# Where the split tokens lie in on-chip memory: four small constants placed ahead of them, and a column offset for blocks of two tiles

## The chip, the core and the metric

The kernel runs on one core of one Trainium2 chip, in one launch. The metric is the device time of that launch in microseconds: 485.12 us is the median of three runs of the kernel before (484.73 to 485.75). The profile that is read below is of one further execution, which took 485.06 us; its trace spans 483.0 us from the first to the last instruction.

## The reference

For 2,048 tokens of width 448 the program computes one block of a conditioned network: six modulation vectors from a condition `c`, a normalised state-space convolution with a gated residual, and then a normalised, modulated feed-forward part with a gated residual. All of it is float32. Cut to what matters here:

```python
mod = (silu(c) @ w_mod)                       # sa, ca, ga, sb, cb, gb
h = layernorm(x) * (1 + ca) + sa
x = x + ga * ssm_conv(h)                      # long convolution over the 2048 tokens
h = layernorm(x) * (1 + cb) + sb
x = x + gb * ((silu(h @ w_gate) * (h @ w_up)) @ w_down)   # 448 -> 1792 -> 448
```

The last line is where nearly all matmuls lie, and the change touches the buffers that hold its `h`.

## The kernel before, in words

The 2,048 tokens are 16 tiles of 128 tokens. They are worked in six blocks (`BLOCKS = [2, 2, 3, 3, 3, 3]`): two blocks of two tiles (256 tokens), then four of three (384 tokens). For each block the modulated, normalised tokens are turned so that the 448 channels lie along the 128 partitions, in four groups `k` (the fourth holds the last 64 channels twice). Each is written as two float32r numbers, a rounded high part and what is left over: `hhi[:, k, :]` and `hlo[:, k, :]`, two buffers of 128 partitions by 4 groups by 384 columns (L140 and L141). These are the "tokens' parts". The function `parts` (L197) writes them, ACT the high part at L198 and DVE the low part at L199; for the first block the functions `high` and `low` do the same at L423 and L428. A block of two tiles uses columns 0 to 255 of each group, a block of three columns 0 to 383.

The feed-forward part runs over 14 slices `f` of 128 hidden units (function `ffn`, from L707). For each slice, `gate_up` forms the gate and the up product. Each is a sum of 11 matmuls in one PSUM bank: seven with `hhi` and four with `hlo` as the operand that streams through TensorE, 256 or 384 columns at a time, all at one line:

```python
pe.matmul(ps[s][:, 0:n], w[:, s, a], (hlo if lo else hhi)[:, k, 0:n], ...)      # L729
```

The stationary operand `w[:, s, a]` is a 128 by 128 piece of `wgu[f]` (named `gu` in the profile), the split weights. So a slice has 22 such matmuls, a block 308 and the program 1,848: 616 in the two blocks of two tiles, 1,232 in the four of three. Each has a different stationary operand from the one before, so that each matmul in the profile has a weight load (LDWEIGHTS, engine PEld) of its own, which runs beside the matmul before it. After the 22 matmuls of slice `f` come the down products of slice `f - 1` at L773: per tile of tokens three matmuls of 448 columns, where the split activations `phi` and `plo` are stationary and the split weights `wdh` and `wdl` stream through. In the last block the last two slices' down products are at L801.

All on-chip buffers are allocated in the order of the code, one behind the other, each at a multiple of 32 bytes in every partition. In the built program `hhi` begins at byte 48,544 and `hlo` at byte 54,688; the weights `gu` of slice 0 begin at byte 63,264, and the other slices' weights lie some whole number of times 512 bytes behind them. The step from one group `k` to the next is 1,536 bytes, and from one piece of weights to the next 512. So, counted modulo 512, every streaming operand of L729 begins at byte 416 and every stationary one at byte 288. At L773 the streaming `wdh` and `wdl` begin at 288 and 32, and the stationary `phi` and `plo` at 288. The matrix `tri` of the scan at L933 to L935 begins at 384.

The order of work is written out by hand in the code; nothing here is decided by a scheduler. The four constants of the change are columns of one number per partition: `ones`, `mhalf` (the exponent -0.5 of the normalisation, read by POOL at L168), `ntok` and `pick`. They are filled in the first microseconds.

Of the kernel before, what the change touches and what calls it, by code (L numbers as in the profile page):

```python
# [8 lines left out]
F32 = mybir.dt.float32  # L9
# [42 lines left out]
def f32(ap):  # L52
    return ap.bitcast(F32)
# [3 lines left out]
def tile_kernel(ctx, tc, x, a_re, a_im, b_re, b_im, c_re, c_im, log_dt,  # L57
                wd, wgate_up, states, groups, vecs, dft, idft, out):
    nc = tc.nc
    sy, ve, sc, po, pe = nc.sync, nc.vector, nc.scalar, nc.gpsimd, nc.tensor  # L60
    ctx.enter_context(tc.manual_schedule())

    const = ctx.enter_context(tc.tile_pool(name="const", bufs=1))
# [7 lines left out]
    def bank():  # L71
        t = psg.tile([128, 512], F32, name="bank")
        return t
# [38 lines left out]
    def split_d(j, part=None):  # L112
        hi, lo = wp[j]
        if not part:
            sc.copy(hi, wdn[j])
        if part != 0:
            ve.tensor_tensor(lo, wdn[j], f32(hi), op=OP.subtract)

    def split_w(j, part=None, en=ve):
        hi, lo, st = wgu[j][:, :, 0:3, :], wgu[j][:, :, 4:7, :], wgu[j][:, :, 3, :]  # L120
        w = raw[j]
        if not part:
            sc.copy(wgu[j][:, :, 0:4, :], w)  # L123
        if part is None or part == 1:
            en.tensor_tensor(lo, w[:, :, 0:3, :], f32(hi), op=OP.subtract)  # L125
        if part is None or part == 2:
            en.tensor_tensor(st[64:128], w[64:128, :, 3, :], f32(st[64:128]), op=OP.subtract)
# [9 lines left out]
    g0 = const.tile([128, D], F32)  # L137
    gm0 = const.tile([128, D], F32)
    gm1 = g0
    hhi = const.tile([128, 4, MB * 128], F32R)  # L140
    hlo = const.tile([128, 4, MB * 128], F32R)  # L141
    gd = const.tile([128, D], F32)
# [54 lines left out]
    def parts(hi, lo, src, k):  # L197
        sc.activation(hi, src, AF.Identity, bias=sbc[:, k:k + 1])  # L198
        ve.scalar_tensor_tensor(lo, src, sbc[:, k:k + 1], f32(hi), op0=OP.add, op1=OP.subtract)  # L199

    def transposes(ts):
        n = len(ts) * 128
        for k in range(4):
            ps = CV if k == 2 else bank()
            for j, i in enumerate(ts):
                pe.transpose(ps[:, j * 128:(j + 1) * 128], xn[i][:, k * 128:(k + 1) * 128], ident)  # L206
            parts(hhi[:, k, 0:n], hlo[:, k, 0:n], ps[:, 0:n], k)

    xd = [dram.tile([128, 512], F32, name=f"xd{q}") for q in range(MB)]

# [9 lines left out]
    def split_turned(ts):  # L220
        n, m = len(ts) * 128, len(ts)
        for k in range(4):
            hi, lo = (h[:, k, 0:n].rearrange("p (q a r) -> p q a r", q=m, a=4) for h in (hhi, hlo))
            parts(hi, lo, turned[:, 0:m, :, k, :], k)

    wp0 = ctx.enter_context(tc.tile_pool(name="wp0", bufs=1))
    ones = const.tile([128, 1], F32)
    mhalf = const.tile([128, 1], F32)
    ntok = const.tile([128, 1], F32)
    cs = const.tile([128, 5], F32)  # L230
    pick = const.tile([128, 1], F32)
    gac = const.tile([128, 4], F32)

    def mod_part(ps, w, ks):
# [34 lines left out]
    with tc.tile_pool(name="pre", bufs=1) as pre:  # L269
# [149 lines left out]

        def high(q, ks=range(4)):  # L420
            for k in ks:
                c_ = slice(q * 128, (q + 1) * 128)
                sc.activation(hhi[:, k, c_], pk[q][:, k * 128:(k + 1) * 128], AF.Identity, bias=sbc[:, k:k + 1])  # L423

        def low(q, ks=range(4)):
            for k in ks:
                c_ = slice(q * 128, (q + 1) * 128)
                ve.scalar_tensor_tensor(hlo[:, k, c_], pk[q][:, k * 128:(k + 1) * 128], sbc[:, k:k + 1], f32(hhi[:, k, c_]),  # L428
                                        op0=OP.add, op1=OP.subtract)

# [9 lines left out]
        def flag_of():  # L440
# [45 lines left out]
            **{f"r{q}": do(n2.root, [q]) for q in range(2)}, **{f"n1{q}": do(norm, q) for q in range(2)},  # L486
            **{f"xn{q}": (lambda q: lambda: sc.activation(h2[q], h2[q], AF.Copy, scale=n2.of[q][1]))(q) for q in range(2)},
            **{f"tr{q}": do(to_channels, q) for q in range(2)}, "hi1": do(high, 1),
            **{f"hi0{z}": do(high, 0, (2 * z, 2 * z + 1)) for z in range(2)},
            "lo1": do(low, 1),  # L490
            **{f"lo0{z}": do(low, 0, (2 * z, 2 * z + 1)) for z in range(2)},

            "w0": do(split_w, 0, 0), "w01": do(split_w, 0, 1, WV), "w02": do(split_w, 0, 2, WV),
# [211 lines left out]
    def run_blocks(pools, stages, first=None):  # L705
        work, hid = pools.work, pools.hid
        def ffn(ts, fresh, last, todo):  # L707
            n = len(ts) * 128
# [3 lines left out]
            def gate_up(f, nw):  # L712
                head = fresh and f < 2
                if fresh and f:
                    split_d(f)
                w = wgu[f]
                p = hid.tile([128, 256], F32, name="p") if fresh else p_of[f % 2]
                hi = hid.tile([128, MB * 128], F32R, name="phi")
                lo = hid.tile([128, MB * 128], F32R, name="plo")
                ps = [DN[2] if fresh and f == 0 else bank(), bank()]  # L720

                top = [(k, a) for k, ws in enumerate(((0, 4), (1, 5), (2, 6), (3,))) for a in ws]
                low = [(k, k) for k in range(4)]

                def mm(s, ka, lo, first=False, end=False):
                    for q, (k, a) in enumerate(ka):
                        pe.matmul(ps[s][:, 0:n], w[:, s, a], (hlo if lo else hhi)[:, k, 0:n],  # L729
                                  start=first and q == 0, stop=end and q == len(ka) - 1)  # L730

                if head:
                    for k in range(3):
                        for s in range(2):
                            mm(s, [(k, k)], False, k == 0)
                    for s in range(2):
                        mm(s, [(k, 4 + k) for k in range(3)] + [(3, 3)], False)
                    for s in range(2):
                        mm(s, low, True, False, True)
                else:  # L740
                    for s in range(2):
                        mm(s, top, False, True)
                        mm(s, low, True, False, True)
                sc.activation(p[:, 0:n], ps[0][:, 0:n], AF.Silu)  # L744
                pp[f] = hi, lo
                if last and f == NF - 1:
                    c_ = [slice(q * 128, (q + 1) * 128) for q in range(len(ts))]
                    for q in range(len(ts) + 1):
                        for o in c_[q:q + 1]:
                            ve.tensor_tensor(ps[1][:, o], p[:, o], ps[1][:, o], op=OP.mult)  # L750
                            sc.copy(hi[:, o], ps[1][:, o])
                        for o in c_[max(q - 1, 0):q]:
                            ve.tensor_tensor(lo[:, o], ps[1][:, o], f32(hi[:, o]), op=OP.subtract)
                    return
                if nw is not None:
                    split_w(nw, 0)
                ve.tensor_tensor(ps[1][:, 0:n], p[:, 0:n], ps[1][:, 0:n], op=OP.mult)  # L757
                if nw is not None:
                    split_w(nw, 1)
                sc.copy(hi[:, 0:n], ps[1][:, 0:n])  # L760
                ve.tensor_tensor(lo[:, 0:n], ps[1][:, 0:n], f32(hi[:, 0:n]), op=OP.subtract)  # L761
                if nw is not None:
                    split_w(nw, 2)
# [11 lines left out]
            m = len(ts) - 1  # L775
# [64 lines left out]
        if first is not None:  # L840
            for i in TILES[1]:
                load_x(i)
            for i in TILES[0]:
                first(i)
                n2.stat(i, TILES[0])
            n2.root(TILES[0])
            for q, i in enumerate(TILES[0]):
                make_xn(i, work.tile([128, 512], F32, name=f"xn{q}"))
            transposes(TILES[0])
        for b, ts in enumerate(TILES):  # L850
            todo = {}
            if b + 1 < len(TILES):
# [32 lines left out]
                if late:  # L885
                    go(late[0], n2.root, nx)
                    for q, (h, i) in enumerate(zip(late[1], nx)):
                        go(h, make_xn, i, xn_of[q])
                at(NF - 1, 0, transposes if late else split_turned, nx)
            ffn(ts, b == 0, b + 1 == len(TILES), todo)  # L890

# [154 lines left out]
def build(nc, aps, out):  # L1046
    with tile.TileContext(nc) as tc:
        a = dict(aps)
        tile_kernel(tc, a["A_u"].rearrange("b l d -> (b l) d"), *[a[n] for n in _INS[1:] + ["B_w_gate_up", "A_states", "w_mod_groups", "c_log_dt", "dft", "idft"]],
                    out.rearrange("b l d -> (b l) d"))  # L1050
# [20 lines left out]
```

## Time and profile before

| what | value |
|---|---|
| median of three runs | 485.12 us (484.73 to 485.75) |
| the profiled execution | 485.06 us |
| its span, first to last instruction | 483.0 us, so 2.06 us lie around it |
| granted TensorE clock over the span | 0.999 |
| PE busy | 471.6 us (98%) |
| PEld, DVE, ACT, POOL busy | 444.9, 285.1, 155.4, 59.8 us |
| share of PE in the chain that ended last | 92% |
| of it the matmuls of L729 / of L773 | 59% / 28% |

Times are microseconds, unless marked ns. PE is TensorE's matmul, PEld its weight load. The profile gives a matmul a duration that covers its way through the array; successive matmuls overlap, so what one costs is the distance from its start to the next one's. The chain of work that ended last gives that distance: a piece "PE bank L729 x22" is the time that 22 matmuls in a row held the chain. The view of one line gives the shortest, the median and the longest duration of its instructions in ns.

### The profile page before, as it was taken

What the parts mean: (1) busy time and instruction counts of PE and PEld (TensorE: products, weight loads), DVE (VectorE), ACT (ScalarE), POOL (GpSimd) and SP (SyncE); (2) the same over time, 40 slices, a digit from 0 to 9 for tenths busy, and PEclk for the clock granted to TensorE, in tenths of its full rate; (3) what the DMA queues carried; (4) which work ended last, traced back from release to release, by engine and by line L of the source; (5) the groups of instructions that cost most, each with busy time, mean ns of one, the idle gap of its engine ahead of it and who ended that gap; (6) DMA issues with size and microseconds to landing.
All of it is one profiled execution on the core that took longest, in us unless ns stands there. A gap on an engine that the chain in (4) does not pass through costs nothing.

```text
span 483.0 us, 7024 instructions
## 1 busy us (share of the span) xinstructions
PE 471.6 (98%) x2743; PEld 444.9 (92%) x2743; DVE 285.1 (59%) x550; ACT 155.4 (32%) x336; POOL 59.8 (12%) x82
## 2 busy tenths in 40 slices
PE   6999999999999999999999999999999999999995
PEld 4668988999999999999999999999999999999995
DVE  4879998768876546573644757375475544221225
ACT  5876545522234222332312323331222232112111
POOL 1220000000000040310022221002241000000000
PEclk9999999999999999999999999999999999999999
DMA  8965563020001200111200011130001112000001
GB/s 307 405 225 165 194 188 103 0 96 2 1 2 39 58 1 0 45 38 51 92 25 0 2 44 46 43 115 0 2 2 44 45 43 77 22 1 0 1 1 62
DMA packets 18778, 31.24 MB, mean 65 GB/s; under 512 B 2608, under 2 KB 13488, under 8 KB 18736
## 3 DMA queue, kind: packets, MB, share of 16 engines
q1 hardware_dynamic: 18000, 30.52, 18.8%
q8 instruction: 23, 0.38, 0.3%
q10 hardware_dynamic: 736, 0.19, 0.2%
q14 instruction: 19, 0.16, 0.1%
HBM read 24.61 MB, written 6.03 MB: 63 GB/s over the span
## 4 chain that ended last, share of the span: by engine, by line
PE 92%; DMA 3%; DVE 2%; ACT 1%; issue 0%; POOL 0%; SPq 0%; ACTq 0%; DVEq 0%
PE bank L729 59%; PE dn L773 28%; DMA wm<-in_w_mod_groups_dram 2%; DMA x<-in_A_u_dram 1%; PE bank L238 1%; PE dn L449 1%; PE bank L934 1%; PE cv L933 1%; PE cv L935 0%; PE bank L947 0%; DVE x L812 0%; PE bank L206 0%; PE cv L946 0%; PE cv L948 0%; ACT raw L195 0%
## 5 line engine op out<-in xcount | busy, mean ns | idle before, releaser
L729 PE MATMUL bank<-hhi,gu 128*128 128x384 f32 (+1 forms) x1169 | 211.3, 320 | 0.0
L729 PEld LDWEIGHTS bank<-hhi,gu 128*128 128x128 f32 x1169 | 191.2, 188 | 3.1 <-issue 0.7
L729 PE MATMUL bank<-hlo,gu 128*128 128x384 f32 (+1 forms) x668 | 131.8, 319 | 0.0
L757 DVE TENSOR_TENSOR bank<-raw,bank 128x384 f32<-128x384 f32 (+1 forms) x69 | 36.9, 534 | 125.0 <-PE bank L729 121.6
L729 PEld LDWEIGHTS bank<-hlo,gu 128*128 128x128 f32 x668 | 110.2, 188 | 0.0
L760 ACT CAST phi<-bank 128x384 fp32r<-128x384 f32 (+1 forms) x83 | 36.9, 444 | 141.6 <-DVE bank L757 141.6
L744 ACT ACTIVATE raw<-bank 128x384 f32<-128x384 f32 (+1 forms) x70 | 32.9, 470 | 123.0 <-PE bank L729 114.9
L761 DVE TENSOR_TENSOR plo<-bank,phi 128x384 fp32r<-128x384 f32 (+1 forms) x83 | 42.5, 512 | 37.1 <-ACT phi L760 37.1
L773 PE MATMUL dn<-wdh,phi 128*128 128x448 f32 x218 | 58.3, 368 | 0.6 <-DVE run L698 0.4
L773 PE MATMUL dn<-wdh,plo 128*128 128x448 f32 x218 | 57.7, 366 | 0.0
L773 PE MATMUL dn<-wdl,phi 128*128 128x448 f32 x218 | 57.6, 365 | 0.0
L773 PEld LDWEIGHTS dn<-wdl,phi 128*128 128x128 f32 x218 | 41.0, 188 | 3.4
L773 PEld LDWEIGHTS dn<-wdh,plo 128*128 128x128 f32 x218 | 40.9, 188 | 3.3
L773 PEld LDWEIGHTS dn<-wdh,phi 128*128 128x128 f32 x218 | 38.9, 188 | 2.9 <-DVE run L698 0.7
L167 POOL TENSOR_SCALAR rsb<-mvb 128x1 f32<-128x1 f32 (+2 forms) x13 | 4.6, 354 | 171.9 <-DVE mvb L151 171.9
L167 POOL TENSOR_SCALAR rsa<-mva 128x3 f32<-128x3 f32 (+1 forms) x6 | 2.4, 396 | 116.1 <-DVE mva L151 116.1
L123 ACT CAST gu<-raw 128x1024 fp32r<-128x1024 f32 x14 | 14.6, 1046 | 0.0
L125 DVE TENSOR_TENSOR gu<-raw,gu 128x768 fp32r<-128x768 f32 x14 | 13.3, 953 | 0.1
L922 DVE TENSOR_TENSOR vl<-m,vh 128x448 fp32r<-128x448 f32 x12 | 9.1, 757 | 6.7 <-ACT vh L921 6.1
L908 POOL TENSOR_TENSOR m<-m,gm 128x448 f32<-128x448 f32 x9 | 10.4, 1154 | 21.4 <-DVE m L184 17.5
L194 ACT ACTIVATE raw<-raw,rsb 128x64 f32<-128x64 f32 x14 | 4.8, 346 | 21.0 <-DVE raw L193 11.9
L927 POOL TENSOR_TENSOR m<-m,gd 128x448 f32<-128x448 f32 x9 | 11.6, 1284 | 0.0
(232 smaller groups left out, 411.0 us busy)
## 6 DMA issues: line engine op xcount, KB each, us to landing
raw<-in_B_w_gate_up_dram SPq DMA_DIRECT2D x14, 512.0 KB, 3.9
rawd<-in_B_w_down_dram SPq DMA_DIRECT2D x16, 224.0 KB, 4.1
x<-in_A_u_dram SPq DMA_DIRECT2D x12, 224.0 KB, 3.3
out_dram<-x SPq DMA_DIRECT2D x11, 224.0 KB, 2.0
xd<-raw SPq DMA_DIRECT2D x9, 256.0 KB, 2.0
raw<-xd SPq DMA_DIRECT2D x36, 64.0 KB, 2.0
wm<-in_w_mod_groups_dram SPq DMA_DIRECT2D x5, 448.0 KB, 8.2
wm<-in_w_mod_groups_dram SPq DMA_DIRECT2D x5, 336.0 KB, 8.2
```

Of the source, the lines that this page charges most:

```text
L123: sc.copy(wgu[j][:, :, 0:4, :], w)
L125: en.tensor_tensor(lo, w[:, :, 0:3, :], f32(hi), op=OP.subtract)
L167: po.tensor_scalar(rs[:, 0:n], self.mv[:, 0:n, 1], EPS, None, op0=OP.add)
L729: pe.matmul(ps[s][:, 0:n], w[:, s, a], (hlo if lo else hhi)[:, k, 0:n], start=first and q == 0, stop=end and q == len(ka) - 1)
L744: sc.activation(p[:, 0:n], ps[0][:, 0:n], AF.Silu)
L757: ve.tensor_tensor(ps[1][:, 0:n], p[:, 0:n], ps[1][:, 0:n], op=OP.mult)
L760: sc.copy(hi[:, 0:n], ps[1][:, 0:n])
L761: ve.tensor_tensor(lo[:, 0:n], ps[1][:, 0:n], f32(hi[:, 0:n]), op=OP.subtract)
L773: pe.matmul(dn[q][:, 0:D], u[:, cs], v, start=f == 0 and z == 0, stop=f == (NF - 3 if last else NF - 1) and z == 2)
L908: (ve if on_v else po).tensor_tensor(v, h, g, op=OP.mult)
L922: ve.tensor_tensor(vl, v0, f32(vh), op=OP.subtract)
L927: (ve if on_v else po).tensor_tensor(h, h, gd, op=OP.mult)
```

## The change

The four constants are allocated ahead of `hhi` and `hlo`, where before they stood behind them. Four times 32 bytes move `hhi` and `hlo`, and the three buffers directly behind them (`gd`, `sbc`, `flag`), up by 128 bytes, and `cs` up by 32; everything from `gac` on stays where it was. In addition blocks of two tiles keep their parts in columns 48 to 303 of each group, in place of 0 to 255: 192 bytes further. So in the built program, modulo 512, the streaming operands of L729 begin at byte 32 in blocks of three tiles and at byte 224 in blocks of two, with the stationary ones still at 288. Nothing else of the program differs: on each engine the same instructions stand in the same order, with the same waits.

```diff
+    ones = const.tile([128, 1], F32)
+    mhalf = const.tile([128, 1], F32)
+    ntok = const.tile([128, 1], F32)
+    pick = const.tile([128, 1], F32)
+
+    first_col = lambda n: 48 if n == 256 else 0
     hhi = const.tile([128, 4, MB * 128], F32R)
     hlo = const.tile([128, 4, MB * 128], F32R)
     gd = const.tile([128, D], F32)
...
+        c_ = slice(first_col(n), first_col(n) + n)
...
-            parts(hhi[:, k, 0:n], hlo[:, k, 0:n], ps[:, 0:n], k)
+            parts(hhi[:, k, c_], hlo[:, k, c_], ps[:, 0:n], k)
...
-            hi, lo = (h[:, k, 0:n].rearrange("p (q a r) -> p q a r", q=m, a=4) for h in (hhi, hlo))
+            hi, lo = (h[:, k, first_col(n):first_col(n) + n].rearrange("p (q a r) -> p q a r", q=m, a=4) for h in (hhi, hlo))
...
-    ones = const.tile([128, 1], F32)
-    mhalf = const.tile([128, 1], F32)
-    ntok = const.tile([128, 1], F32)
     cs = const.tile([128, 5], F32)
-    pick = const.tile([128, 1], F32)
...
         def high(q, ks=range(4)):
             for k in ks:
-                c_ = slice(q * 128, (q + 1) * 128)
+                c_ = slice(48 + q * 128, 176 + q * 128)
...
         def low(q, ks=range(4)):
             for k in ks:
-                c_ = slice(q * 128, (q + 1) * 128)
+                c_ = slice(48 + q * 128, 176 + q * 128)
...
-                        pe.matmul(ps[s][:, 0:n], w[:, s, a], (hlo if lo else hhi)[:, k, 0:n],
+                        pe.matmul(ps[s][:, 0:n], w[:, s, a], (hlo if lo else hhi)[:, k, first_col(n):first_col(n) + n],
                                   start=first and q == 0, stop=end and q == len(ka) - 1)
```

## The prediction, made before the changed kernel ran

> **What bounds the kernel now.** I read the page's busy shares first, then the chain of waits, and then one slice of each kind of block in the chain in order of time.
>
> ```profile
> span 483.0 us, 7024 instructions
> PE 471.6 (98%) x2743; PEld 444.9 (92%) x2743; DVE 285.1 (59%) x550; ACT 155.4 (32%) x336; POOL 59.8 (12%) x82
> ...
> PE 92%; DMA 3%; DVE 2%; ACT 1%; issue 0%; POOL 0%; SPq 0%; ACTq 0%; DVEq 0%
> ```
>
> TensorE holds 92% of the chain that ended last. A busy PE alone would not say so, since matmul durations overlap, but the chain counts from release to release. DVE, the next engine, is busy 59% of the span. So a nanosecond more or less on every matmul reaches the end almost undiminished. What one matmul costs is read from the chain in order of time. These are two slices of the first kind of block (two tiles, 256 columns), with a piece of the scan in between:
>
> ```profile
> 67.08 2.80 PE bank L729 x22
> 69.88 1.22 PE dn L773 x6
> 71.10 2.60 PE bank L729 x22
> 73.70 0.21 PE bank L945
> 73.91 0.76 PE cv L946 x2
> ```
>
> and this is one slice of the second kind (three tiles, 384 columns):
>
> ```profile
> 303.04 3.87 PE bank L729 x22
> 306.90 1.83 PE dn L773 x9
> 308.73 3.87 PE bank L729 x22
> ```
>
> Columns are the start, the length and what held the chain. A matmul of L729 with 384 columns costs 3.87 us / 22 = 175.9 ns, one with 256 columns 2.60 us / 22 = 118.2 ns, and one of L773 with 448 columns 1.83 us / 9 = 203.3 ns. The chain is tight: nothing stands between these pieces. L946 is a plain float32 matmul of 448 columns, and its two passes take 0.76 us, 380 ns each. If such a pass spends exactly two clocks on a column (my estimate; the row does not say it), a clock is 0.424 ns, and the bare streaming would be 163 ns for 384 columns, 109 ns for 256 and 190 ns for 448. The float32r matmuls are then about 13, 10 and 13 ns above bare streaming, each with its own weight load running beside it. Over 1,232 matmuls of 384 columns and 616 of 256 that is 16.0 + 6.2 = 22.2 us: all that a better place of an operand could ever give back.
>
> **The change part by part.** The instructions, their order and their waits are the same on every engine. Only byte positions move, so every price here is a duration that changes, and no instruction or DMA is added or moved past another.
>
> *The four constants, and gd, sbc, flag and cs.* Nothing but a start address changes for their few readers. I cost it at nothing: most are read by DVE and POOL instructions, and those two engines hold 2% and 0% of the chain (`pick` and `cs` are operands of a few matmuls in the first 33 us). If POOL's reading of `mhalf` became slower by a tenth, it would stay inside the time in which POOL is idle (88% of the span).
>
> *Writing the parts.* ACT at L198 and DVE at L199 write the same numbers 128 bytes further, or 320 bytes in blocks of two.
>
> ```profile
> 150.28 0.33 PE bank L206 x3
> 150.61 2.44 PE dn L773 x12
> 153.05 7.72 PE bank L729 x44
> ```
>
> Between two blocks the down products of the last slices (2.44 us here) stand in the chain while the parts are written, and the next block's matmuls follow without a gap. So I cost this at nothing, too; the cover would have to fall away before a slower write showed, and there are only five such seams.
>
> *Reading the parts, the one term that can count.* All 1,848 matmuls of L729 stream from another place relative to the weights that are loaded beside them: modulo 512 the distance from the stationary to the streaming operand is 128 now; it becomes 256 in blocks of three, and 448 in blocks of two. The trace of before has no row at those distances for L729, so the price has to be bounded. The view of L729 shows how much matmuls of one shape differ now, in a stretch of block 1 (256 columns) and of block 3 (384 columns); the three numbers are the shortest, the median and the longest duration in ns:
>
> ```profile
> L729 PE MATMUL bank<-hhi,gu x171: 274/281/287, 95.0 to 142.0; 128*128 128x256 f32 x171
> L729 PE MATMUL bank<-hlo,gu x96: 278/281/285, 95.9 to 140.4; 128*128 128x256 f32 x96
> ...
> L729 PE MATMUL bank<-hhi,gu x196: 334/337/343, 234.5 to 311.6; 128*128 128x384 f32 x196
> L729 PE MATMUL bank<-hlo,gu x110: 336/337/343, 235.7 to 311.9; 128*128 128x384 f32 x110
> ```
>
> All of these have the same relative place modulo 512, and still differ by up to 13 and 9 ns. Something in the meeting of the stream with the weight load costs a varying amount, and its share can shrink or grow when the two start from another distance. The ends: if every matmul became as quick as the fastest of its kind, three-tile blocks would gain 1,232 x 3 ns = 3.7 us and two-tile blocks 616 x 3 to 7 ns = 1.8 to 4.3 us, together 5.5 to 8.0 us. If every one became as slow as the slowest, they would lose 1,232 x 6 = 7.4 and 616 x 6 = 3.7, together 11.1 us. One row goes further down. In the scan, `vl` streams 448 columns while the next weights are loaded, mostly in 358 ns, and L773 streams the same shape in 365:
>
> ```profile
> L935 PE MATMUL cv<-vl,tri x12: 358/358/367, 116.1 to 376.8; 128*128 128x448 f32 x12
> ...
> L773 PE MATMUL dn<-wdl,phi x218: 358/365/369, 40.4 to 469.3; 128*128 128x448 f32 x109
> L773 PE MATMUL dn<-wdh,plo x218: 362/365/369, 40.8 to 469.9; 128*128 128x448 f32 x109
> ```
>
> There the streaming operand stands 256 bytes, modulo 512, from the next stationary one, the distance that three-tile blocks of L729 get. Seven ns on all 1,848 matmuls would be 12.9 us. Against it stands that `wdl` over `phi` at L773 has this very distance and a median of 365, as much as `wdh` over `plo` at distance 0; the short ones of L935 directly follow a load of `tri`, which starts from a different place. So the row shows that such a matmul can be had 7 ns cheaper, and not that the distance alone does it.
>
> I take a small gain, about half of the way from the median to the fastest: 1.5 ns for each three-tile matmul (half of 337 - 334), and 2 ns for each two-tile one (about half of the 3 to 7 ns). That is 1,232 x 1.5 = 1.85 us and 616 x 2 = 1.23 us, in sum 3.1 us. It is a choice between a gain of 12.9 us and a loss of 11.1, near the rows in the middle. The sum against the profiled execution: 485.06 - 3.1 = **482.0 us**; this execution stands 0.06 us below the median of the three runs, so the same number serves for the median.
>
> Nothing is late next: the engine that waits for these matmuls is ACT at L744 and DVE at L757, and both wait for PE, not PE for them.
>
> ```profile
> L757 DVE TENSOR_TENSOR bank<-raw,bank 128x384 f32<-128x384 f32 (+1 forms) x69 | 36.9, 534 | 125.0 <-PE bank L729 121.6
> L744 ACT ACTIVATE raw<-bank 128x384 f32<-128x384 f32 (+1 forms) x70 | 32.9, 470 | 123.0 <-PE bank L729 114.9
> ```
>
> DVE sits idle 121.6 us waiting for L729 ahead of its product, ACT 114.9 us; a few us less of that turn into nothing new.
>
> **A rule to weigh.** The rows say that a float32r matmul with a load beside it costs some 13 ns more than bare streaming. The Trainium skill, TensorE: Matmul & The Clock Gate, section "Step-by-step: what each phase is for", says the opposite of a collision: "Loading the next tile's weights doesn't steal SBUF read bandwidth from the running matmul", since PE has two read ports. By that rule the place of either operand could not matter, and the time would stay 485.1 us. This trace neither proves the cause of the 13 ns nor shows a matmul of L729 at another place. The rule is the first rival below.
>
> **The rivals.** *The place does not matter* (485.1 us, between 484.1 and 486.1). The surplus is then a fixed price of a weight load, and the scatter is a beat that evens out. For it speak the equal medians of L773 at distances 0 and 256, and the 256-column matmuls of the final down products at L801, which stream `wdh` and `wdl` at distances 0 and 256, too:
>
> ```profile
> L801 PE MATMUL cv<-wdl,phi x2: 282/282/282, 476.2 to 477.2; 128*128 128x256 f32 x2
> L801 PE MATMUL cv<-wdh,plo x2: 282/282/282, 476.4 to 477.3; 128*128 128x256 f32 x2
> ```
>
> 282 ns, where L729 has 281 at distance 128. Against it speaks L935, and that these are six matmuls. Distances that are not a multiple of 128, such as the 448 of two-tile blocks, are hardly seen.
>
> *The new places meet more often: slower* (487.6 us). The same mechanism with the other sign, at L729 alone. In three-tile blocks the surplus becomes slightly larger, +0.8 ns on 1,232 matmuls = 1.0 us; in two-tile blocks the new distance moves half of the way to the slowest, about 2.5 ns on 616 = 1.5 us. It decides as soon as the three-tile median is at 338 and the two-tile one at 283 or more. For it speaks that the slowest lie twice as far from the median as the fastest in three-tile blocks (343, 337, 334): most phases have more to lose than to win. Against it speaks L935.
>
> *A large gain* (about 475 us): most of the L935 step, 5.5 ns, on all 1,848 matmuls is 10.2 us. It needs one distance to be good for the whole load, which the equal medians of L773 contradict.
>
> That the change does not do what it says can hardly be: the positions are fixed in the built program.
>
> **How the numbers follow.** A measurement of this kernel can tell about 0.2%, or 1 us, from no change. I give the small gain 0.45 (477 to 484.1 us), the large one 0.10, no effect 0.18 and the slower case 0.27, of which 0.07 lie above 488. The small gain is likeliest because the spread inside one shape shows that the meeting of stream and load has a price that is not fixed, and one row shows it lower. Faster by over 0.2% is then 0.45 + 0.10 = 0.55, within 0.2% 0.18, slower 0.27. The range of 477 to 488 us leaves out the large gain and the far end of the loss, 0.17 in all; the forecast's own range is 477 to 484.1.
>
> **What would show it.** In the profile of the changed kernel the chain's pieces of 22 matmuls should shrink from 3.87 to about 3.84 us in blocks of three, and from 2.60 to about 2.56 us in blocks of two; the medians of L729 go to about 335.5 and 279. L773 must stay at a median of 365, since none of its operands moves, and L198 and L199 at their durations. I am wrong if the medians of L729 stay at 337 and 281 (no effect), if either rises, or if the time moves while L729 does not: then something other than the reading of the parts is at work.

## The result and the profile after

The changed kernel took **481.91 us** (median of six runs, 480.99 to 483.51), the kernel before 485.09 us in six runs of its own. The ratio is 0.9937, with a 95% interval of 0.9920 to 0.9954: faster by 0.6%. The forecast was 482.0 us. The profiled execution took 480.99 us, the fastest of the six, with a span of 479.0 us; 0.9 us of what the two profiles differ by is therefore scatter between runs, and 0.6 us of it lies ahead of the first gate matmul, which starts at 33.0 us in place of 33.5 (in the profiles of the other kernels below it starts anywhere from 33.3 to 34.4).

The busy shares and the chain of waits after the change are almost those of before. The six inserted lines move L729 to L732, L773 to L776, L935 to L938.

```profile
PE 469.2 (98%) x2743; PEld 440.7 (92%) x2743; DVE 284.9 (59%) x550; ACT 155.2 (32%) x336; POOL 59.4 (12%) x82
...
PE 93%; DMA 3%; DVE 1%; ACT 1%; issue 0%; SPq 0%; ACTq 0%; DVEq 0%
```

TensorE bounds as before, and only its matmuls have other prices. The chain in order of time, first in a block of two tiles and then in a block of three:

```profile
69.87 2.52 PE bank L732 x22
```

```profile
231.89 7.63 PE bank L732 x44
239.52 1.85 PE dn L776 x9
```

22 matmuls of 256 columns take 2.52 us in place of 2.60, and 44 of 384 columns 7.63 us in place of 2 x 3.87 = 7.74. But nine down products, of which no operand moved, take 1.85 us in place of 1.83. The views of the two lines, shortest, median and longest duration in ns: L732 in a stretch of block 1 and one of block 3, as in the prediction, and L776 over the whole run:

```profile
L732 PE MATMUL bank<-hhi,gu x177: 276/277/285, 93.8 to 141.0; 128*128 128x256 f32 x177
...
L732 PE MATMUL bank<-hlo,gu x100: 276/277/285, 94.1 to 140.3; 128*128 128x256 f32 x100
```

```profile
L732 PE MATMUL bank<-hhi,gu x190: 333/334/347, 232.8 to 308.4; 128*128 128x384 f32 x190
...
L732 PE MATMUL bank<-hlo,gu x111: 334/334/339, 232.9 to 308.9; 128*128 128x384 f32 x111
```

```profile
L776 PE MATMUL dn<-wdl,phi x218: 362/368/372, 39.9 to 465.3; 128*128 128x448 f32 x109
...
L776 PE MATMUL dn<-wdh,plo x218: 358/368/371, 40.3 to 465.9; 128*128 128x448 f32 x109
```

Before, the medians were 281, 337 and 365. Not only is the median of the gate and up products lower, it now nearly coincides with the shortest: where the starts before followed each other in a beat (in one three-tile block: 173, 174, 175, 182, 176 ns, over and over), after the change they run at 173, 173, 174.

The two-tile blocks are less even than one piece shows. Within one block of the changed kernel, with all operands in one and the same place, twelve slices can be read alone by their starts. 22 matmuls take 2.50 to 2.52 us in seven of them and 2.59 in the five that begin between 115 and 131 us:

```profile
110.91 2.52 PE bank L732 x22
...
115.25 2.59 PE bank L732 x22
...
139.31 2.51 PE bank L732 x22
```

From the starts of successive matmuls, leaving out steps of over 215 ns (seams and waits), the mean price is, in ns:

| matmul | before | after | x count | us |
|---|---|---|---|---|
| gate and up, two tiles (256 columns) | 118.9 | 115.1 | 616 | -2.3 |
| gate and up, three tiles (384 columns) | 176.0 | 173.7 | 1,232 | -2.8 |
| down (448 columns) | 203.4 | 205.4 | 654 | +1.3 |

Together that is -3.8 us; the left-out steps in the blocks give back 0.4, and with the 0.6 us ahead of the first gate matmul it makes the 4.0 us between the two spans. In three-tile blocks alone the down products go from 203.3 to 205.7 ns; that number is used from here on.

### The profile page after: what moved, and what is told of

It reads as the page before. It is cut to its first block, busy times and chain, and to the rows that moved or that the text cites. A ratio compares the mean times of both kernels' runs of the same rounds, so it can differ in the third digit from the quotient of the medians.

```text
span 479.0 us, 7024 instructions
## 1 busy us (share of the span) xinstructions
PE 469.2 (98%) x2743; PEld 440.7 (92%) x2743; DVE 284.9 (59%) x550; ACT 155.2 (32%) x336; POOL 59.4 (12%) x82
## 4 chain that ended last, share of the span: by engine, by line
PE 93%; DMA 3%; DVE 1%; ACT 1%; issue 0%; SPq 0%; ACTq 0%; DVEq 0%
PE bank L732 58%; PE dn L776 28%; DMA wm<-in_w_mod_groups_dram 2%; DMA x<-in_A_u_dram 1%; PE dn L452 1%; PE bank L241 1%; PE bank L937 1%; PE cv L936 1%; PE cv L938 0%; PE bank L950 0%; PE bank L251 0%; PE bank L377 0%; DVE x L815 0%; PE bank L213 0%; PE cv L951 0%; PE cv L949 0%
## 5 line engine op out<-in xcount | busy, mean ns | idle before, releaser
L732 PE MATMUL bank<-hhi,gu 128*128 128x384 f32 (+1 forms) x1169 | 208.1, 316 | 0.0
L732 PEld LDWEIGHTS bank<-hhi,gu 128*128 128x128 f32 x1169 | 189.1, 188 | 3.4 <-issue 0.7
L732 PE MATMUL bank<-hlo,gu 128*128 128x384 f32 (+1 forms) x668 | 129.7, 316 | 0.0
L760 DVE TENSOR_TENSOR bank<-raw,bank 128x384 f32<-128x384 f32 (+1 forms) x69 | 36.9, 534 | 122.8 <-PE bank L732 119.1
L732 PEld LDWEIGHTS bank<-hlo,gu 128*128 128x128 f32 x668 | 108.4, 188 | 0.0
L776 PE MATMUL dn<-wdh,phi 128*128 128x448 f32 x218 | 58.6, 369 | 0.6 <-DVE run L701 0.5
L776 PE MATMUL dn<-wdh,plo 128*128 128x448 f32 x218 | 58.2, 368 | 0.0
L776 PE MATMUL dn<-wdl,phi 128*128 128x448 f32 x218 | 58.1, 367 | 0.0
L776 PEld LDWEIGHTS dn<-wdl,phi 128*128 128x128 f32 x218 | 40.9, 188 | 3.9
L776 PEld LDWEIGHTS dn<-wdh,plo 128*128 128x128 f32 x218 | 40.9, 188 | 3.9
L776 PEld LDWEIGHTS dn<-wdh,phi 128*128 128x128 f32 x218 | 38.6, 188 | 2.9 <-DVE run L701 0.7
L173 POOL TENSOR_SCALAR rsa<-mva 128x3 f32<-128x3 f32 (+1 forms) x6 | 2.4, 397 | 115.2 <-DVE mva L157 115.2
```

Of the source, the lines that this page charges most:

```text
L173: po.tensor_scalar(rs[:, 0:n], self.mv[:, 0:n, 1], EPS, None, op0=OP.add)
L776: pe.matmul(dn[q][:, 0:D], u[:, cs], v, start=f == 0 and z == 0, stop=f == (NF - 3 if last else NF - 1) and z == 2)
```

## The experiments

Below, **distance** is the byte at which the streaming operand begins less that of the stationary one, modulo 512, as laid out in the built programs. Two theories stood at the start. By the distance theory the price of a matmul is set by this number, since the stream meets the weight load that runs beside it. By the place theory it is set by where the streaming operand lies in itself. A third says that any move disturbs the beat and nothing follows from a number. All means are taken as in the table above.

**The two parts of the change alone.** First the constants without the column offset:

```diff
-    first_col = lambda n: 48 if n == 256 else 0
+    first_col = lambda n: 0
...
```

> The constants lie ahead (streaming parts 128 bytes further), but two-tile blocks begin at column 0 again. Distance modulo 512 from weights to parts: 256 in all blocks. Distance theory (a matmul's price is set by the distance between its streaming operand and the weights loaded beside it): three-tile pieces of 22 stay at the changed kernel's 3.82 us; two-tile pieces leave the changed kernel's 2.50 us, to an unknown value between 2.49 and 2.72. If 256 is good for any width: 2.50 and about 482 us. Place theory (the absolute place of the streaming operand alone sets it): the same three-tile pieces, two-tile unknown. Luck theory (any move breaks the beat and nothing follows from the distance): three-tile pieces anywhere from 3.80 to 3.90.

Measured: 484.21 us, ratio 0.9977 (0.9968 to 0.9987). Three-tile matmuls at 173.7 ns, as in the changed kernel; two-tile ones at 119.9, a little worse than before. So the same 128 bytes that help 384 columns do not help 256. The chain in a block of two tiles, and in one of three:

```profile
49.48 2.63 PE bank L732 x22
```

```profile
244.55 3.82 PE bank L732 x22
248.37 1.85 PE dn L776 x9
```

Then the 48 columns without the constants, which stand behind the parts again:

> Columns 48 to 303 in two-tile blocks, but the constants behind the parts as before. Distances: 128 in three-tile blocks as before, 320 in two-tile ones. Distance theory: three-tile pieces of 22 back at 3.87 us, and the down products beside them back at 1.83 us for nine; two-tile pieces between 2.49 and 2.72 us; in all about 483 to 485.5 us. Luck theory: three-tile pieces need not come back to 3.87.

Measured: 484.99 us, ratio 0.9995 (0.9980 to 1.0009). Three-tile matmuls are back at 176.0 ns and the down products between them at 203.3; two-tile ones, now at distance 320, have 117.9:

```profile
49.76 2.59 PE bank L731 x22
...
244.61 3.87 PE bank L731 x22
```

The offset of 48 columns is thus worth 1 ns by itself and 4.8 ns on top of the 128 bytes: it is not the column that counts, but where the sum ends. The granted clock is no rival: it was 0.997 with the constants alone and 1.000 with the columns alone, where three-tile matmuls are the slower ones.

**A whole 512 bytes.** In the kernel before, the identity matrix is allocated behind the parts:

```diff
-    ident = const.tile([128, 128], F32)
     tri = const.tile([128, 128], F32R)
...
     hlo = const.tile([128, 4, MB * 128], F32R)
+    ident = const.tile([128, 128], F32)
```

> The kernel before with the 128 by 128 identity allocated behind the parts, so that the parts move down by exactly 512 bytes; every distance modulo 512 is as before. Distance theory with a period of 512 bytes or a divisor of it: all pieces as before (3.87, 2.61, 1.83 us) and 485.1 us within 0.5. Place theory with a longer period, or luck: other values, by up to 3 us.

Measured: 485.04 us, ratio 1.0001 (0.9986 to 1.0016). The means are 119.0, 176.0 and 203.3 ns, and the beat of the three-tile blocks runs through the same values. Moving the parts does nothing if it is by 512 bytes:

```profile
49.00 2.61 PE bank L729 x22
...
244.24 3.87 PE bank L729 x22
```

**Moving the weights instead.** The changed kernel, with its parts where the change put them, and everything behind them 128 bytes further:

```diff
     gac = const.tile([128, 4], F32)
+    pad = const.tile([128, 32], F32, name="pad")
```

> The changed kernel with 128 unused bytes ahead of all weights and the split activations. The parts stay where the change put them (32 and 224 modulo 512), and everything that is stationary at the gate and up products moves 128 bytes, so the distances are 128 and 320, as in the kernel with the columns alone. Distance theory: three-tile pieces go back to 3.87 us, two-tile ones to the value of that kernel, the time as there (483 to 485.5 us). Place theory: pieces stay at 3.82 and 2.50 us and the time near 481.9.

Measured: 484.69 us, ratio 0.9993 (0.9984 to 1.0003). The gain is gone, with the parts at their new place:

```profile
244.09 3.88 PE bank L733 x22
247.97 1.82 PE dn L777 x9
```

Three-tile matmuls cost 176.2 ns and two-tile ones 118.1, within 0.2 ns of the values that distances 128 and 320 have in the kernels before and with the columns alone, and not those of the place (173.7 and 115.1). The place theory falls here, and the luck theory with it: three kernels that set distance 128 in three-tile blocks, each in another way, came back to 176.0, 176.0 and 176.2 ns. The split down weights and the split activations moved along with the weights here; the activations are moved alone further below, the split down weights nowhere.

**A scan of distances.** Four kernels, each run once and profiled in that run, beside one run of the kernel before at 485.33 us. `gd` goes ahead of the parts for 256 bytes, the constants for 128, unused columns ahead of the weights or of the split activations take 64 to 128 off, and the two blocks of two tiles each get a column of their own, so that a kernel tries up to four distances:

```diff
-    first_col = lambda n: 48 if n == 256 else 0
+    gd = const.tile([128, D], F32)
+    first_col = lambda ts: {0: 16, 2: 48}.get(ts[0], 0)
...
```

> The constants and gd ahead of the parts: distance 0 in three-tile blocks; the first block begins at column 16 (distance 64), the second at column 48 (192). The down products' operands keep their distances of 0 and 256. If the distance counts modulo 256, three-tile pieces are 3.82 us as at 256, and the second block's 2.50 to 2.53 us as at 448; the first block's about 2.60 as at 320. If it counts modulo 512, these may be anything between 3.76 and 3.90 and between 2.46 and 2.66. Carry-over theory (a down product's price depends on the beat that the gate and up products leave): nine down products take 1.85 us if the three-tile pieces are locked at one even value, 1.83 if they beat; own-distance theory: 1.83 whatever the gate and up products do, which the runs so far speak against.

Measured: 482.70 us. Three tiles at 0: 173.8 ns, the same as at 256, with down products at 205.7, again the same. Two tiles at 64: 118.0, as at 320; at 192: 115.9, about as at 448. All three pairs say that the distance counts modulo 256. The three-tile piece:

```profile
243.20 3.82 PE bank L732 x22
```

> gd ahead of the parts, the constants behind: distance 384 in three-tile blocks and in the first block, 480 in the second (column 24). The split activations lie 64 bytes further from the split down weights: distances at the down products 448 and 192. Modulo 256: three-tile pieces 3.87 us and the first block 2.61 as at 128; the second block near the 2.50 of 448 if a good place is wide, near 2.6 if it is narrow. Down products: own-distance theory expects another value than 203.5 ns, between 193 and 210; carry-over alone expects 203.5 as beside every three-tile beat so far.

Measured: 484.59 us. In a block of three:

```profile
244.42 3.87 PE bank L731 x22
```

At 384, three tiles 175.9 and two tiles 119.2, both as at 128, a fourth pair. At 480, two tiles 118.2: 32 bytes beside 448 most of the gain is gone. The down products at 448 and 192 cost 201.9 ns, less than in any kernel up to here, though the three-tile matmuls beside them beat as before.

> The constants ahead and 64 unused bytes ahead of the weights: distance 192 in three-tile blocks; first block at column 80 (distance 0), second at column 56 (416). Split activations 128 bytes further: distances 384 and 128 at the down products. If a place that is good for one width is good for the other, three-tile pieces fall below 3.82 us here, as 448 (the same modulo 256) did for two tiles; if each width has its own, they stay between 3.82 and 3.90. First block: 2.63 as at 256 if the period is 256. Second block: between 2.50 and 2.60, beside 448. Down products 193 to 210 ns by their own distance, 203.5 or 205.5 by carry-over alone.

Measured: 483.61 us. Three tiles at 192: 174.4; two tiles at 0: 120.1, at 416: 119.1. The place that is best for 256 columns is neither the best nor the worst for 384. Down products at 384 and 128: 203.4 ns.

> gd ahead, the constants behind, 64 unused bytes ahead of the weights: distance 320 in three-tile blocks; the first block at column 36 (464), the second at column 28 (432), 16 bytes to either side of 448. Split activations 96 bytes further: distances 416 and 160 at the down products. A wide good place: 2.50 us in both blocks; a narrow one: above 2.55 on one side at least. Three-tile pieces between 3.76 and 3.90 us: distance 320 gave two tiles a value between the best and the worst, so about 3.85. Down products as in the two kernels with other distances there.

Measured: 480.89 us. In a block of three:

```profile
243.04 3.81 PE bank L732 x22
```

Three tiles at 320: 173.4, steady, the lowest found; my "about 3.85" for their pieces was a miss, since two tiles have only a middling value at this distance. Two tiles at 464: 117.6, at 432: 119.0. So 16 bytes to either side of 448 cost most of the gain or all of it. Down products at 416 and 160: 201.7.

**The best of each.** Three-tile distance 320, two-tile 448, down products 416 and 160:

```diff
+    gd = const.tile([128, D], F32)
+    first_col = lambda ts: {0: 32, 2: 32}.get(ts[0], 0)
...
+    pad = const.tile([128, 16], F32, name="pad")
...
+            self.gap.tile([128, 24], F32, name="gap")
```

The first two lines replace those of the changed kernel, with the four constants behind the parts again; `pad` stands ahead of the weights and `gap` ahead of the split activations.

> The best distance found for each of the three kinds of matmul, counted modulo 256: 64 in three-tile blocks (320), 192 in two-tile blocks (448, column 32), 160 at the down products (416 and 160). Distance theory: two-tile pieces of 22 at 2.50 to 2.53 us, three-tile ones at 3.82, nine down products at 1.81 to 1.82; two blocks shorter by about 1.3 us in all than in the kernel with columns 36 and 28, so about 479.5 us, faster than the changed kernel by 2 to 3 us. If the gains don't add up (each good place moves the beat of its neighbour), about 481 us.

Measured: **479.64 us**, ratio 0.9882 (0.9863 to 0.9901), below the changed kernel's interval. In its trace the starts in a block of two tiles, gate and up products from 100.95 to 103.48:

```profile
100.95 0.98 PE L732 MATMUL bank<-hhi,gu 128*128 128x256 f32 x7
...
103.48 0.57 PE L776 MATMUL dn<-wdh,phi 128*128 128x448 f32 x2
```

2.53 us for 22. And in a block of three, from the chain:

```profile
241.81 3.81 PE bank L732 x22
245.63 1.82 PE dn L776 x9
```

The means are 115.2 and 173.4 ns for gate and up products, and 201.7 for the down products. The gains add up: about 479.5 us was expected.

**Where the slower down products come from.** Two kernels differ from this one in the place of the split activations alone.

> As the kernel with the best distances, but the split activations 64 bytes lower: distances 480 and 224 at the down products (224 modulo 256). Own-distance theory: another value than 201.6 ns there, between 198 and 206, with the gate and up pieces as in the kernel with the best distances. Nothing known says better or worse.

Measured: 480.53 us, ratio 0.9900 (0.9875 to 0.9924); down products 204.1 ns, the gate and up products beside them 173.5. The down products, too, have a price by their own distance: 160 gives 201.7, 224 gives 204.1.

> As the kernel with the best distances, but without the bytes ahead of the split activations: distances 0 and 256 at the down products, as in the kernels before and changed. Gate and up products as in the kernel with the best distances (locked at 173.4 ns). Carry-over theory: down products at 205.5 ns as beside every locked three-tile piece at these distances, nine of them 1.85 us, and the time 654 x 3.9 ns = 2.5 us above the kernel with the best distances. If the slower down products came from the distance 256 or 0 of the gate and up products and not from the locked beat: 203.5 ns and 1.2 us above.

Measured: 479.79 us, ratio 0.9903 (0.9870 to 0.9936). The gate and up products are as even as in the best kernel, but the down products do not cost 205.5 ns. In the view of their line, in three-tile blocks:

```profile
L776 PE MATMUL dn<-wdl,phi x38: 362/365/369, 240.2 to 309.9; 128*128 128x448 f32 x38
...
L776 PE MATMUL dn<-wdh,plo x36: 362/365/368, 240.8 to 305.0; 128*128 128x448 f32 x36
```

Their mean is 202.1 ns. My carry-over theory as I had put it, that an even run of the matmuls ahead makes the down products dear, falls: 173.4 ns and even, and still cheap. So does the other reading with 203.5.

The starts show what the two prices are made of. In the changed kernel, in blocks of three, the first of nine down products takes 201 ns and each of the other eight 206 or 207; in this kernel, with the same distances of 0 and 256 and the same even run ahead, they go round 201, 202, 203, 199, 207, 203, 202, 203, 199. So the down products have a beat of their own, and it can lock, too, but here at a dear value.

## Why the prediction was right, and where not

*The bound and the only term.* Both held. The instructions and waits are the same, PE holds 93% of the chain, and what is not scatter lies in what a matmul costs. The writing of the parts stayed as it was: the high part's 384-column form has a median of 606 ns before and after, the low part's 612 and 614.

*The mechanism.* The prediction took the scatter within one shape as a sign that the meeting of stream and weight load has a price that can change with the distance. The four runs on the parts and on the moves of 512 and 128 bytes show that the distance sets it in three-tile blocks, where every kernel at one distance has the same mean within 0.3 ns. In two-tile blocks the distance decides which values can occur, and not always which of them does: 2.50 and 2.59 us for 22 stand in one block. That it is the weights and not the split activations is shown: moving the latter by 64 or 96 bytes left the three-tile matmuls at 173.4 to 173.5 ns. Whether it is the load beside the matmul that is met, or the matmul's own earlier one, cannot be told within a slice, where both lie at the same place modulo 256. The last matmul of a slice tells more: the load that runs beside it is that of `phi`. From its start to that of the first down product it is 173 to 174 ns in three-tile blocks of the kernel with the best distances and of the one without bytes ahead of the split activations, but 180 in every slice of the one with `phi` 64 bytes lower, though the six steps before it are 173 to 174 in all three. So the place of the load beside it counts for that step. By which mechanism stays open.

*The sizes.* Three-tile matmuls were forecast to gain 1.5 ns and gained 2.3; two-tile ones 2 and gained 3.8. Both are nearer to the whole step from the median to the fastest (3, and 3 to 7 ns) than to half of it, because in the starts of the changed kernel the beat locks at a low value (173 to 174 ns, in most two-tile slices 113 to 114) and no longer visits the slow ones. The two-tile mean of 115.1 ns takes in the slices at 2.59 us. With these two terms alone, 2.8 + 2.3 = 5.1 us, the profiled time of before would have become 480.0 us. Of the 22.2 us that the prediction estimated as the most that places could give back, the best kernel here reached 5.4 (485.02 us for the kernel before beside it, less 479.64).

*The step that failed* is the sentence that L773 must stay at a median of 365 since none of its operands moves. It went to 368, and 654 times 2.0 ns gave back 1.3 of the 5.1 us that the gate and up products gained. The right total comes from gains that were taken too small and a loss that was left out, so that it was met to 0.1 us is luck. A down product's price hangs on its own distance and on that of the matmuls ahead of it: in three-tile blocks, at the same own distances of 0 and 256, it is 202.7 to 203.3 ns behind distance 128, 205.7 behind 0 or 256, and 202.1 behind 320. What it is that one line hands to the next stays open: the even steps ahead are 173 to 174 ns in the changed kernel and in the one at 202.1 alike. The signs that the prediction named, the median durations, are not the price either. In the kernel with the best distances the median is 336 ns, above the changed kernel's 334, though its matmuls follow each other faster (173.4 against 173.7 ns):

```profile
L732 PE MATMUL bank<-hhi,gu x168: 336/336/338, 241.6 to 308.4; 128*128 128x384 f32 x168
```

*The rivals.* "The place does not matter" is refuted by the four runs above. It leaned on equal medians at distances 0 and 256, and on L801 at the same two; with a period of 256 bytes these are one distance, and the argument had compared a place with itself. With its parts at the same place, a 384-column matmul costs 173.7 or 176.2 ns by the place of its weights. The Trainium skill (TensorE: Matmul & The Clock Gate, "Step-by-step: what each phase is for") says that loading the next tile's weights takes no SBUF read bandwidth from the running matmul. What the prediction drew from that, that the place of either operand could not matter, does not hold for these float32r matmuls; whether read bandwidth is what they share is not shown. "Slower" was right in one thing: the constants alone do make two-tile matmuls slower, by 1.0 ns at distance 256, and it is the column offset that turns this round. The row of L935, which the prediction gave as a hint, has not moved:

```profile
L938 PE MATMUL cv<-vl,tri x12: 358/358/369, 113.7 to 373.3; 128*128 128x448 f32 x12
```

Its operands were not moved either, so it says nothing on the cause.

## What to carry to other kernels

Where a stream of float32r matmuls bounds and each has its own weight load, read the distance between the starts of successive matmuls; a repeating uneven beat above the bare streaming time (163 ns for 384 columns by the prediction's estimate) is worth a scan of where the streaming operand begins relative to the weights, in steps of 16 to 32 bytes over 256, for each width apart. Align nothing by feel: the best place for one width is an ordinary one for another, and a good place can make the next line's matmuls dearer, so the sum is what to measure. Read the slices one by one, too, since one mean can cover two values. And before two equal rows are read as "no effect", make sure that they differ in the quantity in question modulo its likely period.

## What the runs showed of the hardware that was not expected

The mean step from start to start, in ns, by distance modulo 256. A range is over several kernels or blocks.

| distance | 256 columns | 384 columns |
|---|---|---|
| 0 | 119.8 to 120.1 | 173.7 to 173.8 |
| 64 | 117.8 to 118.3 | 173.4 to 173.5 |
| 128 | 118.9 to 119.2 | 175.9 to 176.2 |
| 160, 176 | 119.1, 119.0 | not tried |
| 192 | 114.8 to 116.3 | 174.4 |
| 208, 224 | 117.6, 118.2 | not tried |

At some distances a block settles at one even value and at others it goes round a beat of several values. At 192 the 256-column matmuls have both: the range of 114.8 to 116.3 is, seams apart, a mixture of slices at 2.50 to 2.53 us and slices at 2.59. Either can last over several slices. In the changed kernel the dear one began at 115 us, behind a tile of the scan, and ended at 134 us, behind another; in the kernel without bytes ahead of the split activations it holds in about half of the slices. What sets it off was not tried.
